# Features dealt to partitions by four, in a kernel of attention with memory beside a SiLU layer

## The chip, the cores and the metric

The kernel runs on one core of a Trainium2 chip. The metric is device time in microseconds (us), from one launch. Five engines have their own instruction queues: TensorE (PE in the profile; its weight loads are PEld), VectorE (DVE), ScalarE (ACT), GpSimd (POOL) and SyncE (SP), which issues most of the DMAs.

## What is computed

The input x has 2048 rows of 512 features in bf16. Each row is normed, and two layers read the normed rows:

```python
xn = _layernorm(x, axis=-1)
return x + _A_ref(xn, A_wq, A_wk, A_wv, A_wo, A_beta) + _B_ref(xn, B_w1, B_w2)

# A: 32 heads of 16, 4 segments of 512 rows; in each segment, with M and z summed over the segments before
q, k, v = xn @ wq, xn @ wk, xn @ wv                 # split in heads and segments
p = softmax(q @ k.T * scale + mask);  a_dot = p @ v
a_mem = (phi(q) @ M) / (phi(q) @ z + 1e-6)          # phi(t) = t + 1 where t > 0, else exp(t)
o = g * a_mem + (1 - g) * a_dot                     # g = sigmoid(beta), one value a head
M += phi(k).T @ v;  z += phi(k).sum(rows)
# A's result is o @ wo;  B's is silu(xn @ w1) @ w2, w1 of 512x1792
```

A sum over the 512 features of xn is the same in whatever order the features are taken, as long as xn and the rows of the weight are in the same order. The change rests on this.

## The kernel before

Rows of x are taken in 16 tiles of 128 rows; four tiles make a segment. All weights stay in SBUF. A product over 512 features takes four steps of 128 features, one feature to a partition, so that both sides are stored as 128 partitions by 4 chunks. `xnT` holds the normed rows turned that way, for all 2048 rows; `wq_sb`, `wk_sb`, `wv_sb` and `w1_sb` hold the weights. Feature f stands at partition f modulo 128 in chunk f div 128. A load of wk (L168 to L174) thus moves, for each partition, four rows of the weight that lie 128 rows apart: runs of 1 KB. wv comes in two loads of two chunks. w1 comes in two halves of its columns (L176 to L180), in runs of 1792 bytes.

The path of a tile into `xnT`:

- sums of the row on VectorE (L286, L289);
- one over the root of the variance: for tiles 0 to 3 on ScalarE and VectorE (L303, L306), one tile at a time; for later tiles four at a time on GpSimd (L297, L300);
- the norm, `ln_norm` (L313 to L318), one VectorE instruction that reads 128x512 bf16 and writes the tile `xn_t`;
- the turn. Tiles 0 to 3 go through TensorE: `turn_mm` (L840 to L845) makes four transposes of 128x128 into PSUM, and `turn_copy` (L847) copies the result to `xnT` on ScalarE or VectorE. Tiles 4 to 15 are turned by a DMA that SP issues, `turn_far` (L856, L857).

After that come the products of q, k, v and h (h is the layer with w1), in `product` (L333 to L343): one instruction over the whole array (L336), or four on 32 columns each (L338). Scores go to PSUM (L724), ScalarE makes their exponentials (L730), GpSimd clears what the mask takes away (L744), and L791 sums v with them. GpSimd also splits k into even and odd heads (L385). VectorE copies the products out of PSUM (L376 for k, L399 for q, L406 for v, L821 and L828 for the weighed sums) and multiplies h by its gate (L497), each of which frees one of the four PSUM banks that these products share.

The order of all this is written out by hand in the string `ORDER` (L16 to L90): words that are run one after the other, so that each engine's queue has its instructions in that order. `Nv6` is the norm of tile 6 on VectorE, `XD6` its turn by DMA, `X0.1` a turn on TensorE, `h0.2.0` a part of a product of h for segment 0, `hv0.0` its gating, `kp0.1` a split of k on GpSimd. The norms stand in this order there:

```text
Nv0 .. Nv1 .. Nv2 .. Nv3 (start)   Nv6 Nv4 XD6 XD4 .. Nv5 XD5 (behind S2, S1)   Nv7 (S3)
Nv8 Nv10 XD8 (S10)   Nv9 Nv11 XD11 (S13)   Nv15 XD15 (S24)   Nv14 (S18)   Nv12 .. Nv13 (S23, S30)
```

At the start SP issues tiles 0 and 2 of x, the two loads of wv, wk, wq, tiles 4 to 7 of x, the two halves of w1, and the rest of x; ScalarE issues tiles 1 and 3, and much later w2 and wo.

Of the kernel before, what the change touches and what calls it, by code (L numbers as in the profile page):

```python
# [93 lines left out]
def kernel(  # L94
# [13 lines left out]
    nc = tc.nc  # L108

    P = 128  # L110
    S = 2048
    D = 512
    DT = D // P
# [5 lines left out]
    TPS = L // P  # L119
# [24 lines left out]
    def xs(t0, t1):  # L144
        if t0 >= NT - TPS:
            return x_end[:, t0 - NT + TPS : t1 - NT + TPS, :]
        return x_lo[:, t0:t1, :] if t1 <= TPS else x_hi[:, t0 - TPS : t1 - TPS, :]

    w1_sb = cpool.tile([P, DT, F], BF16, name="w1_sb")
    w2_sb = cpool.tile([P, FT, D], BF16, name="w2_sb")  # L150
    wk_sb = cpool.tile([P, DT, D], BF16, name="wk_sb")
    wq_sb = cpool.tile([P, DT, D], BF16, name="wq_sb")
    wv_sb = cpool.tile([P, DT, D], BF16, name="wv_sb")
# [3 lines left out]
    def load_x(eng, t0, n):  # L157
        eng.dma_start(
            out=xs(t0, t0 + n),
            in_=x_flat[t0 * P : (t0 + n) * P, :].rearrange("(n p) d -> p n d", p=P),  # L160
        )
# [6 lines left out]
    def load_w(eng, w_sb, W, k0, k1):  # L168
        eng.dma_start(out=w_sb[:, k0:k1, :], in_=W.rearrange("(ko ki) n -> ki ko n", ki=P)[:, k0:k1, :])

    load_w(nc.sync, wv_sb, A_wv, 0, 2)
    load_w(nc.sync, wv_sb, A_wv, 2, 4)
    load_w(nc.sync, wk_sb, A_wk, 0, 4)
    load_w(nc.sync, wq_sb, A_wq, 0, 4)  # L174
    load_x(nc.sync, 4, 4)
    for half in range(2):  # L176
        cols = slice(half * F // 2, (half + 1) * F // 2)
        nc.sync.dma_start(
            out=w1_sb[:, :, cols], in_=B_w1.rearrange("(ko ki) n -> ki ko n", ki=P)[:, :, cols]
        )  # L180
    load_x(nc.sync, 8, 4)
    load_x(nc.sync, 12, 4)
# [1 line left out]
        out=beta_r[:], in_=bass.AP(tensor=A_beta.tensor, offset=A_beta.offset, ap=[[1, H], [0, 4], [1, 1]])  # L184
# [6 lines left out]
    ident = cpool.tile([P, P], BF16, name="ident")  # L191
    make_identity(nc, ident[:])
    Vzs = []
    for i in range(2):
# [6 lines left out]
        out=b16[:], in_=ones8[:], compare_op=ALU.is_ge, fill=0.0,  # L201
# [3 lines left out]
        out=b16[:], in_=b16[:], compare_op=ALU.is_ge, fill=0.0,  # L205
# [73 lines left out]
    mv_all = cpool.tile([P, NT, nc.vector.BN_AGGR_DIM], F32, name="mv_all")  # L279
    rstd_all = cpool.tile([P, NT, 1], F32, name="rstd_all")  # L280
# [30 lines left out]
    xn = {}  # L311

    def ln_norm(t, eng):  # L313
        xn[t] = work.tile([P, D], BF16, name="xn_t", tag="x_res", bufs=4)
        eng.tensor_scalar(
            out=xn[t][:], in0=xs(t, t + 1)[:, 0, :], scalar1=mv_all[:, t, 0:1], scalar2=rstd_all[:, t, 0:1],
            op0=ALU.subtract, op1=ALU.mult,
        )  # L318

    def bank(shape, dtype, name):  # L320
        return pp.tile(shape, dtype, name=name, tag="pb")
# [518 lines left out]
    def turn_mm(t, n):  # L840
        ptr = xn["ptr", t] = bank([P, DT, n, P], BF16, "ptr")
        for i in range(n):
            xn_t = xn.pop(t + i)
            for dt in range(DT):
                nc.tensor.transpose(ptr[:, dt, i, :], xn_t[:, dt * P : (dt + 1) * P], ident[:])  # L845

    def turn_copy(t, n, copy):  # L847
        ptr, parts = xn.pop(("ptr", t)), 2 if t < 2 else 1
# [12 lines left out]
    def keep_busy(n):  # L861
# [23 lines left out]
        "sh": half_store, "xl": load_res, "st": out_store,  # L885
        "xs": ln_stats, "xc": ln_sums, "xd": ln_var, "xg": ln_root, "xq": ln_sqrt, "xi": ln_inv, "tb": first_exp,
        "Nv": lambda t: ln_norm(t, nc.vector), "Na": lambda t: ln_norm(t, nc.gpsimd),
        "X": turn_mm, "XD": turn_far, "Xv": lambda t, n: turn_copy(t, n, vec), "Xa": lambda t, n: turn_copy(t, n, act),
        "odd": make_odd, "bmask": make_bmask, "kind": make_kind, "tanh": make_tanh, "gate": make_gate,
        "zeros": make_zeros, "ones": lambda i: nc.gpsimd.memset(Vzs[i][:, :, :, 1, :], 1.0),  # L890
# [52 lines left out]
```

## Time and profile before

| | |
|---|---|
| median of 3 runs | 220.99 us (220.85 to 221.06) |
| the profiled execution | 220.8 us |
| its span, first to last instruction | 219.1 us |
| TensorE, VectorE, ScalarE, GpSimd busy | 211.6, 181.0, 184.2, 126.8 us |
| TensorE's granted clock | 1.000 of full speed |

A profile is one execution. "Busy" counts the time in which an engine has an instruction running. A group's row names line, engine and operation, then output and inputs by the program's names, shapes and count, and the mean time of one. A row of the timeline starts with the start time and the time taken, both in us from the start of the span; in brackets stands how long the engine was idle before, and what ended that. L with a number is a line of the kernel.

### The profile page before, as it was taken

The numbers are of one execution on the slowest core, as the hardware profiler recorded it, in microseconds if no ns is written. First come the engines' busy times: TensorE is split into PE (matmuls) and PEld (weight loads), VectorE is DVE, ScalarE is ACT, GpSimd is POOL, SyncE is SP. The second block draws the span as 40 slices with busy tenths as digits, with TensorE's granted clock in tenths as the row PEclk, the third lists the DMA queues.
The fourth block names the chain that finished last, engine by engine and source line by source line (L and its number), as shares of the span: only waits on it lengthen the run. The fifth ranks groups of instructions, "written<-read, shape, count | busy, mean of one in ns | idle before, by whom it ended". The sixth has DMA issues, their size and how long they took to land.

```text
span 219.1 us, 9343 instructions
## 1 busy us (share of the span) xinstructions
PE 211.6 (97%) x4019; PEld 116.3 (53%) x4042; DVE 181.0 (83%) x370; ACT 184.2 (84%) x173; POOL 126.8 (58%) x203
## 2 busy tenths in 40 slices
PE   7999999999999999999999999999999999999994
PEld 7666655556544544445544445455454544465663
DVE  7899999999897878757988979777899798669364
ACT  3899989999999999999999999999999988860000
POOL 6039986679687845695845486667768473410000
PEclk9999999999999999999999999999999999999999
DMA  6994549242003035321122142160032221322313
GB/s 197 357 372 128 79 129 344 42 79 46 4 4 75 25 86 71 83 62 29 51 74 61 43 121 28 47 79 7 4 99 75 75 76 45 97 60 76 97 52 97
DMA packets 33273, 19.60 MB, mean 89 GB/s; under 512 B 14672, under 2 KB 33232, under 8 KB 33232
## 3 DMA queue, kind: packets, MB, share of 16 engines
q1 hardware_dynamic: 30608, 16.39, 29.1%
q10 hardware_dynamic: 2624, 2.62, 3.7%
q8 instruction: 31, 0.51, 1.0%
q14 instruction: 10, 0.08, 0.1%
HBM read 9.96 MB, written 2.10 MB: 55 GB/s over the span
## 4 chain that ended last, share of the span: by engine, by line
PE 82%; DVE 9%; POOL 4%; issue 2%; ACT 1%
PE ps L336 20%; PE psO L338 16%; PE ps L338 15%; PE psS L724 9%; PE psO L336 9%; PE psV L791 8%; PE psS L338 4%; DVE stats L286 2%; POOL Pb L744 2%; DVE Vz L406 1%; POOL k L385 1%; DVE hT L497 1%; DVE pk L433 1%; POOL lows L744 1%; PE ptr L845 1%
## 5 line engine op out<-in xcount | busy, mean ns | idle before, releaser
L730 ACT ACTIVATE Pb<-psS 128x2048 bf16<-128x2048 f32 x72 | 135.2, 1877 | 6.3 <-PE psS L724 4.1
L744 POOL TENSOR_SCALAR_AFFINE_SELECT Pb<-Pb 128x512 bf16<-128x512 bf16 (+2 forms) x88 | 61.6, 710 | 19.2 <-ACT Pb L730 16.5
L497 DVE SCALAR_TENSOR_TENSOR hT<-th,ps 128x512 bf16<-128x512 bf16 x56 | 38.0, 681 | 10.6 <-ACT th L492 10.2
L744 POOL TENSOR_SCALAR_AFFINE_SELECT lows<-Pb 64x512 bf16<-64x512 bf16 (+1 forms) x40 | 23.2, 581 | 37.5 <-ACT Pb L730 31.1
L338 PE MATMUL psO<-w_sb,hT 128*32 128x512 bf16 (+2 forms) x708 | 43.3, 321 | 0.0
L336 PE MATMUL ps<-xnT,w_sb 128*128 128x512 bf16 (+1 forms) x165 | 34.2, 329 | 0.4 <-DVE Vz L406 0.2
L492 ACT ACTIVATE th<-ps 128x512 bf16<-128x512 f32 x56 | 33.2, 594 | 1.7 <-PE ps L338 1.6
L338 PEld LDWEIGHTS <-hT 128*32 128x32 bf16 x876 | 21.6, 97 | 14.0 <-issue 2.6
L338 PE MATMUL ps<-xnT,w_sb 128*32 128x512 bf16 (+1 forms) x448 | 26.4, 348 | 0.0
L724 PE MATMUL psS<-qT,k 32*128 32x64 bf16 (+3 forms) x512 | 23.0, 233 | 0.5 <-ACT Pb L730 0.3
L336 PEld LDWEIGHTS <-w_sb 128*128 128x128 bf16 x168 | 15.8, 98 | 11.4 <-issue 1.0
L791 PE MATMUL psV<-Pb,Vz 128*32 128x448 bf16 (+7 forms) x512 | 21.6, 286 | 0.2 <-POOL Pb L744 0.2
L724 PEld LDWEIGHTS <-k 32*128 32x128 bf16 x512 | 9.4, 92 | 22.8 <-issue 22.2
L336 PE MATMUL psO<-w_sb,hT 128*128 128x512 bf16 (+2 forms) x82 | 20.9, 326 | 0.6 <-issue 0.5
L791 PEld LDWEIGHTS <-Vz 128*32 128x32 bf16 x768 | 16.2, 97 | 9.2 <-issue 0.8
L621 DVE SCALAR_TENSOR_TENSOR o_out<-psO,x_res 128x512 bf16<-128x512 f32 x14 | 9.6, 689 | 6.6 <-PE psO L338 4.9
L338 PEld LDWEIGHTS <-w_sb 128*32 128x32 bf16 x448 | 11.2, 96 | 7.3 <-issue 1.6
L724 PE MATMUL psS<-qT,kT 16*128 16x448 bf16 (+3 forms) x256 | 14.7, 269 | 0.0
L821 DVE CAST oraw<-psV 128x512 bf16<-128x512 f32 x15 | 10.2, 682 | 3.1 <-PE psV L791 3.0
L406 DVE CAST Vz<-ps 128x512 bf16<-128x512 f32 x15 | 10.2, 682 | 2.8 <-PE ps L338 1.6
L336 PEld LDWEIGHTS <-hT 128*128 128x128 bf16 x89 | 7.8, 98 | 8.7 <-issue 2.2
L336 PE MATMUL ps<-xnT,wq_sb 128*128 128x256 bf16 (+1 forms) x59 | 12.1, 322 | 0.2 <-issue 0.2
(113 smaller groups left out, 333.5 us busy)
## 6 DMA issues: line engine op xcount, KB each, us to landing
spr<-rz SPq DMA_DIRECT2D x56, 64.0 KB
x_res<-in_A_x_dram SPq DMA_DIRECT2D x16, 128.0 KB
out_dram<-o_out SPq DMA_DIRECT2D x15, 128.0 KB
w_sb<-in_B_w_dram SPq DMA_DIRECT2D x2, 896.0 KB
w_sb<-in_B_w_dram ACTq DMA_DIRECT2D x1, 1792.0 KB
x_hi<-in_A_x_dram SPq DMA_DIRECT2D x2, 512.0 KB
wv_sb<-in_A_wv_dram SPq DMA_DIRECT2D x2, 256.0 KB
wk_sb<-in_A_wk_dram SPq DMA_DIRECT2D x1, 512.0 KB
```

Of the source, the lines that this page charges most:

```text
L286: nc.vector.bn_stats(out=stats[t][:], in_=xs(t, t + 1)[:, 0, :])
L336: return [nc.tensor.matmul(out, lhsT=lhsT, rhs=rhs, start=start, stop=stop, skip_group_check=True)]
L338: nc.tensor.matmul(out[c : c + 32], lhsT=lhsT[:, c : c + 32], rhs=rhs, start=start, stop=stop, tile_position=(0, c), skip_group_check=True,)
L406: copy(out=Vzs[s % 2][:, j, :, 0:3:2, :], in_=sts[s].pop(("v", j))[:, :].rearrange("p (h r d) -> p h r d", r=2, d=DH),)
L492: nc.scalar.activation(out=th[:], in_=sts[s]["h", ft][:, :], func=AF.Tanh, scale=0.5)
L497: nc.vector.scalar_tensor_tensor(out=st["hT"][:, ft, :], in0=st.pop(("th", ft))[:], scalar=1.0, in1=st.pop(("h", ft))[:, :], op0=ALU.add, ...
L621: out = nc.vector.scalar_tensor_tensor(out=o_out[:], in0=st.pop(("psO", j)), scalar=0.5, in1=st["x", j][:], op0=ALU.mult, op1=ALU.add)
L724: nc.tensor.matmul(psS[:, g, c : c + q2 - q1], lhsT=keys[rows], rhs=st["qT"][rows, dt, q1:q2], start=True, stop=True, tile_position=(32 * ...
L730: exp = nc.scalar.activation(out=blocks(Pb, b).rearrange("p y g c -> p g y c"), in_=psS[:, :, :].rearrange("p g (y c) -> p g y c", c=BLOCK ...
L744: over[id(Pb)].append(nc.gpsimd.affine_select(out=out, in_=in_, compare_op=ALU.is_ge, fill=0.0, base=base, pattern=[[0, out.shape[1]], [1, ...
L791: nc.tensor.matmul(psV[32 * g : 32 * g + 32, q0 : q0 + nq].rearrange("p (y c) -> p y c", y=weights.shape[2]), lhsT=Vzs[s % 2][:, kt, 4 * d ...
L821: copy(out=oraw[:], in_=sts[s].pop(("psV", 0))[:, :])
```

## The change

The features are dealt out by four: feature f stands at partition f div 4, in chunk f modulo 4. Partition p then holds rows 4p to 4p + 3 of a weight, which lie side by side in memory. wk and wq so come in runs of 4 KB, and each load of wv, of two chunks, in runs of 2 KB. w1 is dealt in the same way, but comes in halves of its columns, so its runs stay at 1792 bytes. w2 and wo, which are not multiplied with xn, keep the old function.

`xnT` has to follow. For tiles 0 to 3 the norm stays, and each transpose on TensorE reads every fourth column of the normed tile in place of 128 neighbours. For tiles 4 to 15 the turn by DMA stays, and the norm on VectorE deals the features: it reads its row of x with a step of four elements and writes the 512 results side by side, in the new order.

```diff
+    def load_wx(eng, w_sb, W, k0, k1):
+        eng.dma_start(out=w_sb[:, k0:k1, :], in_=W.rearrange("(ki ko) n -> ki ko n", ki=P)[:, k0:k1, :])
+
-    load_w(nc.sync, wv_sb, A_wv, 0, 2)
-    load_w(nc.sync, wv_sb, A_wv, 2, 4)
-    load_w(nc.sync, wk_sb, A_wk, 0, 4)
-    load_w(nc.sync, wq_sb, A_wq, 0, 4)
+    load_wx(nc.sync, wv_sb, A_wv, 0, 2)
+    load_wx(nc.sync, wv_sb, A_wv, 2, 4)
+    load_wx(nc.sync, wk_sb, A_wk, 0, 4)
+    load_wx(nc.sync, wq_sb, A_wq, 0, 4)
...
-            out=w1_sb[:, :, cols], in_=B_w1.rearrange("(ko ki) n -> ki ko n", ki=P)[:, :, cols]
+            out=w1_sb[:, :, cols], in_=B_w1.rearrange("(ki ko) n -> ki ko n", ki=P)[:, :, cols]
...
     def ln_norm(t, eng):
         xn[t] = work.tile([P, D], BF16, name="xn_t", tag="x_res", bufs=4)
+        to, frm = xn[t][:, :], xs(t, t + 1)[:, 0, :]
+        if t >= TPS:
+            to, frm = to.rearrange("p (k c) -> p k c", k=DT), frm.rearrange("p (c k) -> p k c", k=DT)
         eng.tensor_scalar(
-            out=xn[t][:], in0=xs(t, t + 1)[:, 0, :], scalar1=mv_all[:, t, 0:1], scalar2=rstd_all[:, t, 0:1],
+            out=to, in0=frm, scalar1=mv_all[:, t, 0:1], scalar2=rstd_all[:, t, 0:1],
             op0=ALU.subtract, op1=ALU.mult,
         )
...
-                nc.tensor.transpose(ptr[:, dt, i, :], xn_t[:, dt * P : (dt + 1) * P], ident[:])
+                nc.tensor.transpose(ptr[:, dt, i, :], xn_t[:, dt:D:DT], ident[:])
```

## The prediction

> **What bounds the kernel now.** I read the page first, then busy time by stretch, then who waited for whom in the start, then single instructions round each norm.
>
> ```profile
> span 219.1 us, 9343 instructions
> PE 211.6 (97%) x4019; PEld 116.3 (53%) x4042; DVE 181.0 (83%) x370; ACT 184.2 (84%) x173; POOL 126.8 (58%) x203
> ```
>
> TensorE is busy for 211.6 of 219.1 us, so 7.5 us is all that waiting costs today. The change adds and removes no product. It can only move the time by making TensorE wait longer or less. The profiled execution took 220.8 us (the span and 1.7 us around it); the median of the runs shown is 220.99, which is 0.19 more.
>
> The busy time by stretch (stretch, length, then busy us of PE, PEld, DVE, ACT, POOL, then clock, DMA share, GB/s) shows what is tight where:
>
> ```profile
> 5.00:9.00 4.00, 3.46 (x35) 2.00 (x34) 3.72 (x15) 2.89 (x9) 0.00 (x0) 1.00 1.02 338
> 10.00:14.00 4.00, 3.84 (x41) 3.12 (x39) 3.22 (x8) 3.71 (x6) 0.77 (x1) 1.00 1.07 382
> 21.00:27.00 6.00, 5.74 (x108) 3.86 (x109) 5.43 (x11) 5.95 (x7) 5.60 (x9) 1.00 0.62 90
> 27.00:38.00 11.00, 10.72 (x204) 5.79 (x204) 10.82 (x22) 10.02 (x11) 8.20 (x13) 1.00 0.74 224
> 46.00:52.00 6.00, 5.97 (x185) 3.46 (x182) 5.59 (x12) 5.95 (x6) 5.76 (x9) 1.00 0.41 70
> ```
>
> In 27 to 38 VectorE has 0.18 us of air in 11, TensorE 0.28. In 46 to 52 TensorE has 0.03 us in 6. The DMA engines are full in the first 14 us. Whether somebody waits for them is told by the waits of TensorE and its weight loads between 5 and 16 us:
>
> ```profile
> PE ptr L845 <- DVE xn_t L315: 0.3, 1, 0.3
> PE psS L724 <- ACT qT L399: 0.2, 1, 0.2
> ```
>
> ```profile
> PEld L845 <- DVE xn_t L315: 1.0, 3, 0.5
> PEld L336 <- ACT xnT L851: 0.8, 2, 0.5
> ```
>
> Every named wait is for a norm (L315) or for a copy out of PSUM (L851, L399). None is for a DMA.
>
> **The loads: 0.** wv, wk and wq are first read here (start, busy time, engine, line):
>
> ```profile
> 6.46 0.11 PEld L336 LDWEIGHTS <-xnT 128*128 128x128 bf16 x2 [0.30 <-ACT xnT L851]
> 8.37 0.37 PEld L336 LDWEIGHTS <-wk_sb 128*128 128x128 bf16 x4
> 10.11 0.86 PEld L336 LDWEIGHTS <-wq_sb 128*128 128x128 bf16 x8
> ```
>
> The product with wv starts when ScalarE's copy ends; those with wk and wq carry no idle time at all. So a load that lands earlier has nobody to release. Nor is it clear that it lands much earlier: 338 GB/s moved in 5 to 9 us, where rows of 1 KB come in, and 382 in 10 to 14, where the 1792-byte runs of w1 take over. The three weights are 1.57 MB: 4.65 us at the one rate, 4.12 at the other, so at most 0.53 us for the last. The bounds are 0 and a gain of 0.53; I take 0, since no row shows a wait that this would shorten. x_hi, w1 and the later rows of x keep their run lengths and come as many as before; SP issues the same DMAs in the same order, so no queue is passed. If the runs are cut into 1 KB pieces all the same, this term stays 0.
>
> **The transposes of the first four tiles: 0.** Sixteen weight loads now read every fourth element.
>
> ```profile
> L845 PEld LDWEIGHTS <-xn_t x16: 95/98/99, 5.6 to 9.0; 128*128 128x128 bf16 x16
> 5.60 0.23 PEld L845 LDWEIGHTS <-xn_t 128*128 128x128 bf16 x4 [0.49 <-DVE xn_t L315]
> ```
>
> Four of them take 0.23 us, one following the other after 0.04. Nothing in this trace loads with a step. Between no change and a load that no longer overlaps the next one (4 x 0.098 = 0.39, so 0.16 more for a tile, 0.64 for four) I take 0, by the row itself. The cover is thin, as TensorE waits for the norm before its tiles and the copies wait for TensorE; the upper end stays in the range.
>
> **The norms of tiles 4 to 15: +0.5.** Tiles 0 to 3 keep their norm as it is. The other twelve read with a step of four. What they take now (ns, min/median/max), and three rows that bear on the rate:
>
> ```profile
> L315 DVE TENSOR_SCALAR xn_t<-x_hi,mv_all,rstd_all x8: 396/406/787, 18.3 to 44.6; 128x512 bf16<-128x512 bf16 x8
> L315 DVE TENSOR_SCALAR xn_t<-x_lo,mv_all,rstd_all x4: 413/414/414, 5.1 to 8.4; 128x512 bf16<-128x512 bf16 x4
> L315 DVE TENSOR_SCALAR xn_t<-x_end,mv_all,rstd_all x4: 632/714/773, 64.1 to 89.5; 128x512 bf16<-128x512 bf16 x4
> ```
>
> ```profile
> L392 DVE TENSOR_SCALAR k<-kT,pm_odd 128x512 bf16<-128x512 bf16 x1 | 0.4, 353 | 0.6 <-ACT kT L376 0.6
> L527 DVE TENSOR_SCALAR zsum<-ps,evec 128x256 f32<-128x256 f32 x1 | 0.5, 484 | 0.0
> L566 DVE TENSOR_SCALAR rz<-ri,gate 32x256 bf16<-32x256 f32 x1 | 0.4, 352 | 0.0
> ```
>
> All three are the same operation with one scalar column. 256 fp32 elements out of PSUM take 484 ns, 256 fp32 elements out of SBUF 352, and 512 bf16 elements out of SBUF 353. So SBUF gains 0.13 us on 256 elements, and packed bf16 passes twice as many in the same time. I read this as one, two and four elements a cycle, with 0.13 us for 128 cycles. Bf16 with gaps between its elements can't be packed, as fp32 can't. Its nearest row is L566: two a cycle, 0.414 + 0.13 = 0.54 us. The ends: 0.41 if nothing is lost, 0.414 + 3 x 0.13 = 0.81 at one a cycle. I take 0.54, so 12 x 0.13 = 1.6 us more of VectorE. What of it reaches TensorE goes by place.
>
> Place A, tiles 6, 4, 5, then 7:
>
> ```profile
> 18.34 1.59 DVE L315 TENSOR_SCALAR xn_t<-x_hi,mv_all,rstd_all 128x512 bf16<-128x512 bf16 x3
> 18.49 0.81 POOL L385 TENSOR_SCALAR k<-kT,pm_odd 128x512 bf16<-128x512 bf16 x1
> 20.44 0.40 DVE L315 TENSOR_SCALAR xn_t<-x_hi,mv_all,rstd_all 128x512 bf16<-128x512 bf16 x1
> 20.91 0.60 PE L336 MATMUL ps<-xnT,w_sb 128*128 128x256 bf16 x4
> 21.11 1.35 DVE L399 CAST qT<-ps 128x512 bf16<-128x512 f32 x2 [0.27 <-PE ps L336]
> 25.49 0.61 PE L338 MATMUL ps<-wv_sb,xnT 128*32 128x512 bf16 x8
> 26.73 0.29 PE L791 MATMUL psV<-Pb,Vz 128*32 128x256 bf16 x4 [0.20 <-POOL Pb L744]
> 27.07 0.69 DVE L821 CAST oraw<-psV 128x512 bf16<-128x512 f32 x1 [0.47 <-PE psV L791]
> ```
>
> ```profile
> L385 POOL TENSOR_SCALAR k<-kT,pm_odd x15: 688/693/1017, 18.5 to 163.0; 128x512 bf16<-128x512 bf16 x15
> ```
>
> Behind the first three norms stands the gating product of h that frees a PSUM bank, done by 20.44; the next product of h starts at 20.91. That is 0.47 us of cover for 3 x 0.13 = 0.39. With the fourth norm VectorE is 0.52 late, of which its idle 0.27 at 21.11 takes half and the 0.47 at 27.07 the rest. The first transpose of these tiles is issued 0.13 later; the product that first reads its tile runs at 25.49, more than 5 us after, and is covered. What isn't covered is GpSimd. Its split of k at 18.49 took 0.81 us beside the norms, while the median of such splits is 0.69; and one of the norms took 0.787, so the two hold each other up. GpSimd is busy for 5.60 of the 6 us from 21 to 27, and at 26.73 TensorE waits for it. One or two norms longer by 0.13 ahead of GpSimd's two splits give 0.13 to 0.26; I take **0.2**.
>
> Place B, tiles 8 and 10, then 9, then 11:
>
> ```profile
> 41.52 0.73 DVE L315 TENSOR_SCALAR xn_t<-x_hi,mv_all,rstd_all 128x512 bf16<-128x512 bf16 x2
> 43.07 0.69 DVE L497 SCALAR_TENSOR_TENSOR hT<-th,ps 128x512 bf16<-128x512 bf16 x1 [0.22 <-ACT th L492]
> 43.67 0.45 DVE L315 TENSOR_SCALAR xn_t<-x_hi,mv_all,rstd_all 128x512 bf16<-128x512 bf16 x1
> 44.64 0.40 DVE L315 TENSOR_SCALAR xn_t<-x_hi,mv_all,rstd_all 128x512 bf16<-128x512 bf16 x1
> 51.83 0.23 DVE L464 COPY M<-psM 128x64 f32<-128x64 f32 x1 [0.37 <-PE ps L338]
> ```
>
> The first pair costs 0.26 and meets 0.22 of idle time; the next two add 0.26. VectorE is then 0.3 us late until its next idle time at 51.83, through the copies of q and k that free the banks, in a stretch where TensorE has 0.03 us of air. I take all of it, **0.3**; the ends are 0 (the banks come free early enough) and 0.5.
>
> Place C, tiles 12 to 15:
>
> ```profile
> 66.31 0.69 DVE L399 CAST qT<-ps 128x512 bf16<-128x512 f32 x1 [0.22 <-PE ps L336]
> 68.70 0.69 DVE L376 CAST kT<-ps 128x512 bf16<-128x512 f32 x1 [0.27 <-PE ps L336]
> 79.06 0.69 DVE L497 SCALAR_TENSOR_TENSOR hT<-th,ps 128x512 bf16<-128x512 bf16 x1 [0.33 <-ACT th L492]
> 91.01 0.69 DVE L497 SCALAR_TENSOR_TENSOR hT<-th,ps 128x512 bf16<-128x512 bf16 x1 [0.81 <-ACT th L492]
> ```
>
> Two norms run at 64 and 65 us, one at 76, one at 89. Each is followed by idle time of at least its 0.13. I take 0, at most 0.1.
>
> The sum is 0 + 0 + 0.2 + 0.3 + 0 = 0.5 us: 221.3 against the profiled 220.8, and 221.5 as a median of runs.
>
> [...]
>
> **The rivals.**
>
> *Faster, 220.5.* The place is the start, the mechanism the landing of wv, wk and wq. A wait is put down to the event that came last; if a weight in truth lands a moment behind the copy that is named, 4 KB runs move it forward. The price: TensorE idles 0.54 us in 5 to 9, and 0.53 is what the faster rate could bring, so -0.5, with the norms hidden. It decides from the point where wk lands after 8.37 or wq after 10.11. For it: DMA share of 1.02. Against it: no wait is put down to a DMA, and both weight loads start without idle time.
>
> *The strided read is slower still, 222.1.* The norm stands between 0.54 and 0.81; in the middle, 0.68, each costs 0.27. A: three make 0.81 against 0.47 of cover, 0.34 late, and some 0.1 for the fourth. B: four make 1.08, less 0.22, of which some 0.6 reaches TensorE before the idle 0.37. C: 0.1. Together 1.1. [...] For it: the step leaves one used element in 8 bytes. At one element a cycle (0.40 each) the same working gives 0.9 + 1.0 + 0.3 = 2.2, 223.2.
>
> *No difference, 221.0.* TensorE's banks and queue ahead take up VectorE's 0.3 in B, and GpSimd is not held longer in A. For it: VectorE is busy for only 83% of the span. Against it: 0.03 us of air.
>
> **How the numbers follow.** The bound is 0.2%, 0.44 us, which is about what a measurement of this kernel can tell from no change: 220.55 to 221.43. Forecast 45%, its own range 221.1 to 222.0; 31 of these lie above the bound and 14 within it. Faster rival 18%, slower read 12%, one a cycle 10%, no difference 15%. Faster: 0.18. Same: 0.14 + 0.15 = 0.29. Slower: 0.31 + 0.22 = 0.53. The range 220.5 to 222.6 holds all but the fastest part of the first rival and the case of one a cycle; the 0.64 for the transposes, on top of the forecast, lies in it.
>
> **What would show it.** The norms of tiles 4 to 15 at about 0.54 us where GpSimd is quiet, those of tiles 0 to 3 at 0.41; weight loads at L845 still near 98 ns; the first products with wv, wk and wq at the same instants; TensorE's idle time up by 0.2 by 27 us and by 0.3 more by 52. The prediction is wrong if the first products with wk or wq start earlier without an earlier copy ahead of them, if the norms take 0.7 or more, or if TensorE's idle time up to 52 us is what it was.

## The result, and the profile after

The changed kernel takes 222.97 us as a median of four runs (222.86 to 223.29), the kernel before 221.03 beside it. The ratio is 1.0091, with a 95% interval of 1.0073 to 1.0108: 1.94 us slower. The profiled execution after took 223.29 us, 2.49 more than that of before; it is the longest of the four, and 0.46 us of what follows is a later start, of which more below.

From the page after, the span, the busy times and the DMA packets; below them the packets of before:

```profile
span 221.6 us, 9343 instructions
PE 212.1 (96%) x4019; PEld 116.4 (53%) x4042; DVE 184.1 (83%) x370; ACT 184.2 (83%) x173; POOL 128.0 (58%) x203
DMA packets 32249, 19.60 MB, mean 88 GB/s; under 512 B 14672, under 2 KB 31696, under 8 KB 32208
```

```profile
DMA packets 33273, 19.60 MB, mean 89 GB/s; under 512 B 14672, under 2 KB 33232, under 8 KB 33232
```

The loads do what they say: 1536 packets of 1 KB have become 256 of 2 KB and 256 of 4 KB, 1024 fewer in all. TensorE does the same work: its busy time is 0.5 us longer (212.1 us against 211.6), its idle time 2.0 (9.5 against 7.5). VectorE is busy for 3.1 us more, where the prediction had 1.6.

Every VectorE instruction stands in the same place of its queue in both kernels, so the start times can be set side by side. Timeline rows after, and those of before that were not shown yet:

```profile
10.88 0.58 ACT L383 CAST kT<-ps 128x512 bf16<-128x512 f32 x1 [0.54 <-PE ps L343]
18.79 2.00 DVE L322 TENSOR_SCALAR xn_t<-x_hi,mv_all,rstd_all 128x512 bf16<-128x512 bf16 x3
28.09 0.69 DVE L828 CAST oraw<-psV 128x512 bf16<-128x512 f32 x1
42.01 0.69 DVE L383 CAST kT<-ps 128x512 bf16<-128x512 f32 x1
54.24 0.23 DVE L471 COPY M<-psM 128x64 f32<-128x64 f32 x1 [0.23 <-PE psM L459]
81.56 0.69 DVE L504 SCALAR_TENSOR_TENSOR hT<-th,ps 128x512 bf16<-128x512 bf16 x1 [0.19 <-ACT th L499]
218.08 0.97 DVE L675 SCALAR_TENSOR_TENSOR o_half<-psS,x_res 128x256 bf16<-128x256 f32 x2 [0.18 <-PE psS L345]
```

```profile
10.42 0.59 ACT L376 CAST kT<-ps 128x512 bf16<-128x512 f32 x1 [0.26 <-PE ps L336]
40.91 0.69 DVE L376 CAST kT<-ps 128x512 bf16<-128x512 f32 x1
215.59 0.97 DVE L668 SCALAR_TENSOR_TENSOR o_half<-psS,x_res 128x256 bf16<-128x256 f32 x2 [0.18 <-PE psS L338]
```

The lag of the changed kernel at these rows is 0.46, 0.45, 1.02, 1.10, 2.41, 2.50 and 2.49 us. It grows in three steps: 0.46 in the start, 0.6 across the norms of tiles 4 to 7, 1.3 across those of tiles 8 to 11. Behind 54 us, with four norms still to come, it hardly moves.

TensorE's own waits between 14 and 55 us name two instructions of VectorE that were not there before, hT and qT (us in total, times, longest):

```profile
PE ps L343 <- DVE hT L504: 1.3, 1, 1.3
PE psS L731 <- ACT Pb L737: 0.6, 2, 0.3
PE ps L343 <- DVE qT L406: 0.5, 1, 0.5
```

In the same stretch before:

```profile
PE psS L724 <- ACT Pb L730: 0.3, 1, 0.3
PE psV L791 <- POOL Pb L744: 0.2, 1, 0.2
PE ps L336 <- DVE Vz L406: 0.2, 1, 0.2
```

The first of the two places, tiles 4 to 7, in the timeline after:

```profile
18.79 2.00 DVE L322 TENSOR_SCALAR xn_t<-x_hi,mv_all,rstd_all 128x512 bf16<-128x512 bf16 x3
18.95 0.94 POOL L392 TENSOR_SCALAR k<-kT,pm_odd 128x512 bf16<-128x512 bf16 x1
21.30 1.44 DVE L322 TENSOR_SCALAR xn_t<-x_hi,mv_all,rstd_all 128x512 bf16<-128x512 bf16 x1
21.37 1.09 POOL L751 TENSOR_SCALAR_AFFINE_SELECT Pb<-Pb 128x1024 bf16<-128x1024 bf16 x1
22.66 1.27 DVE L406 CAST qT<-ps 128x512 bf16<-128x512 f32 x2
23.39 0.81 PE L343 MATMUL ps<-wv_sb,xnT 128*128 128x512 bf16 x2 [0.48 <-DVE qT L406]
```

The norm of tile 7 takes 1.44 us. It starts 0.07 us ahead of a selection of GpSimd (the instruction that clears what the mask takes away) and ends 0.28 us behind it. In the kernel before it took 0.40 at 20.44, and the same selection came 0.14 us later, at 20.58:

```profile
20.58 1.21 POOL L744 TENSOR_SCALAR_AFFINE_SELECT Pb<-Pb 128x1024 bf16<-128x1024 bf16 x1
44.93 0.96 POOL L744 TENSOR_SCALAR_AFFINE_SELECT lows<-Pb 64x512 bf16<-64x512 bf16 x1 [0.96 <-ACT Pb L730]
44.96 0.43 DVE L835 COPY_PREDICATED oraw<-omask,odd 128x256 int32<-128x256 int32 x1
```

There it was GpSimd that gave way: its selections took 1.21 and 0.96 us in place of the usual 1.09 and 0.66. The second place after, tiles 8 to 11:

```profile
44.77 0.80 DVE L322 TENSOR_SCALAR xn_t<-x_hi,mv_all,rstd_all 128x512 bf16<-128x512 bf16 x1
46.02 0.66 POOL L751 TENSOR_SCALAR_AFFINE_SELECT lows<-Pb 64x512 bf16<-64x512 bf16 x1 [0.73 <-ACT Pb L737]
46.09 0.87 DVE L322 TENSOR_SCALAR xn_t<-x_hi,mv_all,rstd_all 128x512 bf16<-128x512 bf16 x1
46.75 1.16 POOL L751 TENSOR_SCALAR_AFFINE_SELECT Pb<-Pb 128x1024 bf16<-128x1024 bf16 x1
46.88 1.32 DVE L842 COPY_PREDICATED oraw<-omask,odd 128x256 int32<-128x256 int32 x1
48.10 0.67 DVE L504 SCALAR_TENSOR_TENSOR hT<-th,ps 128x512 bf16<-128x512 bf16 x1
48.83 1.02 PE L343 MATMUL ps<-xnT,wk_sb 128*128 128x512 bf16 x4 [1.29 <-DVE hT L504]
```

Two norms are held up, at 44.77 and 46.09: 0.80 and 0.87 us, where 0.54 is the time of an undisturbed one. What is held up most is not a norm. It is the merge of odd heads behind them, which copies the sums of the odd heads to their place and which the change doesn't touch: 0.43 us before, 1.32 now. Behind it in VectorE's queue waits the gating of h, and TensorE waits 1.29 us for that.

Last, the instructions that the change altered (ns, min/median/max):

```profile
L322 DVE TENSOR_SCALAR xn_t<-x_hi,mv_all,rstd_all x8: 536/747/1436, 18.8 to 46.1; 128x512 bf16<-128x512 bf16 x8
L322 DVE TENSOR_SCALAR xn_t<-x_lo,mv_all,rstd_all x4: 412/413/414, 5.3 to 8.6; 128x512 bf16<-128x512 bf16 x4
L322 DVE TENSOR_SCALAR xn_t<-x_end,mv_all,rstd_all x4: 762/848/908, 66.6 to 92.0; 128x512 bf16<-128x512 bf16 x4
L852 PEld LDWEIGHTS <-xn_t x16: 111/113/131, 5.8 to 9.5; 128*128 128x128 bf16 x16
```

A stepped norm that nobody disturbs takes 0.536 us. The median of the first eight is 0.747, because five of them run beside GpSimd and take 0.69 us or more.

### The profile page after: what moved, and what is told of

It reads as the page before. It is cut to its first block, busy times and chain, and to the rows that moved or that the text cites. A ratio compares the mean times of both kernels' runs of the same rounds, so it can differ in the third digit from the quotient of the medians.

```text
span 221.6 us, 9343 instructions
## 1 busy us (share of the span) xinstructions
PE 212.1 (96%) x4019; PEld 116.4 (53%) x4042; DVE 184.1 (83%) x370; ACT 184.2 (83%) x173; POOL 128.0 (58%) x203
## 4 chain that ended last, share of the span: by engine, by line
PE 82%; DVE 9%; DMA 5%; issue 2%; ACT 1%
PE ps L343 19%; PE psO L345 16%; PE ps L345 15%; PE psS L731 10%; PE psO L343 9%; PE psV L798 8%; DMA x_hi<-in_A_x_dram 4%; PE psS L345 4%; DVE xn_t L322 3%; DMA x_lo<-in_A_x_dram 1%; DVE stats L290 1%; DVE qT L406 1%; ACT Pb L737 1%; DVE hT L504 1%; DVE Vz L413 1%
## 5 line engine op out<-in xcount | busy, mean ns | idle before, releaser
L392 POOL TENSOR_SCALAR k<-kT,pm_odd 128x512 bf16<-128x512 bf16 x15 | 11.3, 756 | 2.5 <-DVE kT L383 1.6
L343 PE MATMUL ps<-wv_sb,xnT 128*128 128x512 bf16 x41 | 11.5, 380 | 1.0 <-DVE qT L406 0.5
```

The lines of the kernel that those rows point to most:

```text
L343: return [nc.tensor.matmul(out, lhsT=lhsT, rhs=rhs, start=start, stop=stop, skip_group_check=True)]
L392: nc.gpsimd.tensor_scalar(out=to, in0=frm, scalar1=keep[:, 0:1], scalar2=1.0, op0=ALU.mult, op1=ALU.mult)
```

## The experiments

Two theories at first. **P**: the longer norms bring VectorE and GpSimd together at two places, where one waits for a whole instruction of the other. **L**: the loads cost what is lost, since the lag begins in the start. A third, **the rate alone**: twelve norms 0.13 us longer, each passed on in part.

### The three parts alone

Loads only (the changed kernel with the norms and transposes of before), transposes only, norms only (each is the kernel before with that one part of the change), and loads with transposes. In these the features of xn and the rows of the weights no longer match, for some tiles or for all, so only the time counts.

```diff
 # loads only
-        if t >= TPS:
+        if False:
...
-                nc.tensor.transpose(ptr[:, dt, i, :], xn_t[:, dt:D:DT], ident[:])
+                nc.tensor.transpose(ptr[:, dt, i, :], xn_t[:, dt * P : (dt + 1) * P], ident[:])
```

> Only the weights are dealt by four; norms and transposes stay as before, so the rows of a weight meet other features than in the reference. Theory P (the time is lost where VectorE and GpSimd hold each other up behind the longer norms): no wait of that kind can arise, so 0 to +0.5 us against before, all of it in the first 12 us. Theory L (the loads cost what is lost, since wk and wq end later than with 1 KB runs): +0.4 to +1 us, with TensorE waiting for wk at its first product. The rival of the prediction (longer runs land earlier and release TensorE): -0.2 to -0.5 us.

> Only the four transposes of each of the tiles 0 to 3 read every fourth column; weights stay as before, so the first segment's features are not paired as in the reference. In the changed kernel a weight load of these took 113 ns in place of 98. Theory P and theory L: 0 to +0.1 us, as 15 ns times 16 is 0.24 us and most of it lies beside waits for the norm. A theory that the transposes cost the start: +0.3 us or more.

> Only the norms of tiles 4 to 15 read with a step; weights stay as before, so segments 2 to 4 do not pair features as in the reference. Theory P: +1.3 to +2.2 us, most of the 1.94, in two steps behind the norms of tiles 4 to 7 and 8 to 11, with single VectorE instructions of over 1 us there. Theory L: +0.5 us or less. A theory of the rate alone (12 times 0.13 us, each passed on in part): +0.3 to +0.8 us, and no instruction over 1 us.

> The change without the step in the norms; tiles 4 to 15 are then not paired as in the reference. Theory P: 0 to +0.5 us against before. Theory L: +0.8 us or more.

| kernel | median, us | ratio to before | 95% interval |
|---|---|---|---|
| loads only | 221.16 | 0.9997 | 0.9989 to 1.0006 |
| transposes only | 221.08 | 1.0000 | 0.9989 to 1.0010 |
| norms only | 223.01 | 1.0088 | 1.0075 to 1.0101 |
| loads and transposes | 221.05 | 0.9999 | 0.9989 to 1.0009 |

The norms are the whole of it. Theory L falls: packets of 2 and 4 KB change nothing that a run shows, in either direction, and so the faster rival of the prediction falls too. The lag of 0.46 in the start is the spread of single executions. The copy of v ahead of the first of these norms starts at 17.74 us before and at 18.19 after; with the new loads it starts at 17.77 in the kernel with both moves below, with the old ones at 18.46 in that with three pauses, ahead of the first pause. In the profile after, TensorE's weight loads wait once for wk, 0.3 us. They do not in the profiles of loads only and of loads with transposes, which have the same loads, so the wait comes with single executions and not with the length of the runs.

### By place

```diff
 # against norms only
-        if t >= TPS:
+        if TPS <= t < 2 * TPS:        # the other kernel: 2 * TPS <= t < 3 * TPS
```

> The kernel before, with the step in the norms of tiles 4 to 7 only (their segment is then not paired as in the reference). Theory P, by the lag of the changed kernel behind the one before at this place (0.46 us ahead of it, 1.10 behind it): +0.6 us, with the norm of tile 7 at over 1 us beside a selection of GpSimd. Theory of the rate alone (4 of 12 norms): a third of the whole, +0.65, but no instruction over 1 us and no single wait of TensorE over 0.3.

> The same with the step in the norms of tiles 8 to 11 only. Theory P, by the lag at this place (1.10 ahead of it, 2.48 behind it): +1.3 us, with the merge of the odd heads behind the norm of tile 11 held up to over 1 us; less, if the lag from tiles 4 to 7 is needed to bring the two together. Theory of the rate alone: +0.65 us.

Tiles 4 to 7 alone: 221.74 us, ratio 1.0022 (1.0008 to 1.0037), beside 221.10 for before. Tiles 8 to 11 alone: 222.55, ratio 1.0063 (1.0044 to 1.0081). The two differences of medians, 0.64 and 1.45 us (by the ratios 0.5 and 1.4), make 2.09; all twelve made 1.94 and 1.95. So nothing that the runs show is left for tiles 12 to 15, and each place costs its own share without the other. A theory of the rate alone had 0.65 for either: 1.45 speaks against it, 0.64 by itself does not. The long instructions, which it did not have, are there in each, first the timeline of tiles 4 to 7 alone, then that of tiles 8 to 11 alone:

```profile
21.25 1.44 DVE L318 TENSOR_SCALAR xn_t<-x_hi,mv_all,rstd_all 128x512 bf16<-128x512 bf16 x1
```

```profile
46.20 1.32 DVE L838 COPY_PREDICATED oraw<-omask,odd 128x256 int32<-128x256 int32 x1
```

### Moving what is held up

The changed kernel with a word of `ORDER` moved, so that the instruction that is held up has nobody behind it whom TensorE waits for.

```diff
 # norm of tile 7
-S3 ... q0.2.3 Nv7 qv0.2 ha0.1 ...      S4 qv0.3 hv0.1 XD7 ...
+S3 ... q0.2.3 qv0.2 ha0.1 ...          S4 qv0.3 hv0.1 Nv7 XD7 ...
 # merge of odd heads
-... h0.9.1 Om1 h0.9.2 h0.9.3 h0.10.0 ha0.9 hv0.9 kv1.2 kp1.2
+... h0.9.1 h0.9.2 h0.9.3 h0.10.0 ha0.9 hv0.9 kv1.2 Om1 kp1.2
```

> The changed kernel with one word of the order moved: the norm of tile 7 goes behind the copies of q and the gating of h that stood behind it, so that these do not wait when GpSimd holds it up. The same instructions at the same rate. Theory P: 0.4 to 0.7 us less than the changed kernel, 222.3 to 222.6. Theory of the rate alone: as the changed kernel, 222.8 to 223.1, since VectorE has the same work.

> The changed kernel with the merge of odd heads (the instruction that took 1.32 us in place of 0.43) moved behind the gating of h and the copy of k that stood behind it. Theory P: 0.9 to 1.4 us less than the changed kernel, 221.6 to 222.1. Theory of the rate alone: as the changed kernel, 222.8 to 223.1.

> The changed kernel with both moves (norm of tile 7, merge of odd heads). Theory P: the two savings add up, 0.3 + 1.0 below the changed kernel, 221.5 to 221.8, so 0.5 to 0.8 above before; what is left is the first three norms, which hold up GpSimd's splits, and 0.13 us a norm. Theory of the rate alone was not borne out by the single moves; by it nothing would change.

> The kernel before with the same two moves: what the moves do by themselves. Theory P: -0.2 to +0.2 us, since there neither instruction is held up for long. If the moves were a gain of their own: -0.3 us or more, and the savings in the changed kernel would not be put down to the meeting with GpSimd.

| kernel | median, us | ratio to before | 95% interval |
|---|---|---|---|
| changed, norm of tile 7 moved | 222.65 | 1.0075 | 1.0057 to 1.0094 |
| changed, merge moved | 221.99 | 1.0034 | 1.0024 to 1.0044 |
| changed, both moved | 221.63 | 1.0021 | 1.0006 to 1.0035 |
| before, both moved | 221.36 | 1.0002 | 0.9986 to 1.0017 |

The same instructions at the same rate, and 1.4 of the 1.94 us are gone (0.51 are left); in the kernel before the moves gain nothing. The merge is the larger part, as expected. With it alone moved, its own row in the timeline is back to 0.44 us:

```profile
46.31 1.16 POOL L751 TENSOR_SCALAR_AFFINE_SELECT Pb<-Pb 128x1024 bf16<-128x1024 bf16 x1
47.64 0.44 DVE L842 COPY_PREDICATED oraw<-omask,odd 128x256 int32<-128x256 int32 x1
```

The norm of tile 7 gave back less than the 0.4 to 0.7 us expected: 0.32 by the medians, and 0.36 where the merge is moved too. Each time the intervals of the two kernels compared overlap, so its size is not sure. With it out of the way TensorE waits for GpSimd once between 14 and 56 us, 0.2 us, as in the kernel before (at 26.73). GpSimd is late at the first place: its two splits beside the first three norms took 0.94 and 0.63 us, against 0.81 and 0.50 before. The timeline of GpSimd with both moved:

```profile
18.53 0.94 POOL L392 TENSOR_SCALAR k<-kT,pm_odd 128x512 bf16<-128x512 bf16 x1
19.45 0.63 POOL L392 TENSOR_SCALAR k<-kT,pm_even 128x256 bf16<-128x256 bf16 x1
```

### Late, or longer

Is it enough that VectorE comes later, or does it take the longer norm? The kernel before, with norms as short as they were, and small instructions of 0.112 us behind each of the twelve.

```diff
             op0=ALU.subtract, op1=ALU.mult,
         )
+        if t >= TPS:
+            for _ in range(2):        # 1, 2 or 3
+                eng.memset(ident[:], 0.0)
```

> The kernel before, its norms without the step, but each of the twelve is followed by a small instruction that takes VectorE 0.1 to 0.14 us (it clears the identity, which nobody reads any more). If the loss is a matter of when VectorE's instructions meet GpSimd's, whatever made them late: +1.0 to +2.2 us, with the same two instructions held up. If it takes the longer hold of the stepped norm itself: 0 to +0.6 us.

> As the kernel with a pause, but two small instructions behind each norm, since one of them only moved the next instruction by 0.03 to 0.07 us. Wanted are some 0.1 to 0.2 us of delay a norm, as much as the step costs. If being late is enough: +1.0 to +2.2 us, the norm of tile 7 or the merge of odd heads held up to over 1 us. [...]

> The same with three, so that the delay of the step lies between the two or below. If being late is enough: +1.0 to +2.5 us. If it takes the longer norm itself: up to +0.8 us, growing with the delay and without an instruction of over 1 us at the two places.

One pause: 221.35 us, ratio 1.0009 (0.9993 to 1.0024). Two: 222.70, ratio 1.0062 (1.0043 to 1.0081). Three: 224.08, ratio 1.0117 (1.0092 to 1.0141). One pause came out as expected if it takes the longer norm. But it moved the next instruction by only 0.03 to 0.07 us, half of what the step adds or less; two moved it by 0.26, twice the step. Between the two lies the edge, and the timeline shows it. With one pause, VectorE then GpSimd:

```profile
20.72 0.40 DVE L315 TENSOR_SCALAR xn_t<-x_hi,mv_all,rstd_all 128x512 bf16<-128x512 bf16 x1
45.32 0.83 DVE L837 COPY_PREDICATED oraw<-omask,odd 128x256 int32<-128x256 int32 x1
```

```profile
20.83 1.23 POOL L746 TENSOR_SCALAR_AFFINE_SELECT Pb<-Pb 128x1024 bf16<-128x1024 bf16 x1
45.21 0.65 POOL L746 TENSOR_SCALAR_AFFINE_SELECT lows<-Pb 64x512 bf16<-64x512 bf16 x1 [0.96 <-ACT Pb L732]
```

With two:

```profile
20.93 1.12 DVE L315 TENSOR_SCALAR xn_t<-x_hi,mv_all,rstd_all 128x512 bf16<-128x512 bf16 x1
46.41 1.12 DVE L838 COPY_PREDICATED oraw<-omask,odd 128x256 int32<-128x256 int32 x1
```

```profile
20.81 1.09 POOL L747 TENSOR_SCALAR_AFFINE_SELECT Pb<-Pb 128x1024 bf16<-128x1024 bf16 x1
46.14 1.09 POOL L747 TENSOR_SCALAR_AFFINE_SELECT Pb<-Pb 128x1024 bf16<-128x1024 bf16 x1
```

With one pause the norm of tile 7 starts 0.11 us ahead of the selection and takes its 0.40, and GpSimd pays 0.14. With two it starts 0.12 us behind it and takes 1.12. The merge slides from the short selection, which costs it 0.4, onto the long one, which costs it 0.7. With three, the 2.55 us lie just above the upper end of what was expected, and at the second place another instruction loses. The norm of tile 11 waits, and the merge behind it is short:

```profile
47.13 1.10 DVE L315 TENSOR_SCALAR xn_t<-x_hi,mv_all,rstd_all 128x512 bf16<-128x512 bf16 x1
48.62 0.45 DVE L838 COPY_PREDICATED oraw<-omask,odd 128x256 int32<-128x256 int32 x1
```

So being late is enough: a plain norm that comes too late loses as the stepped one does (1.12 us with two pauses, 1.44 with the step). No run makes a plain norm late by just the 0.13 us of the step. That the longer norm, besides, holds GpSimd up is seen in the splits above; how much of the 0.5 us left with both moves is due to that was not told apart.

### The same idea on the kernel before

One sum of the feature map takes 1.03 us at 28.9 us, beside a split of k, where its median is 0.69. It was moved behind two instructions that free banks for TensorE.

```diff
-... vv1.2 fv0.3 O0 Ov0    S11 lw0 hv0.2 xs11 ...
+... vv1.2 O0 Ov0          S11 lw0 hv0.2 fv0.3 xs11 ...
```

> The kernel before with one sum of the feature map (1.03 us at 28.9 us beside a split of k, where its median is 0.69) moved behind two instructions that free banks for TensorE. Theory P, applied to the kernel before: -0.1 to -0.4 us. If the stretch is bound otherwise: 0.

221.47 us, ratio 1.0014 (0.9999 to 1.0029): no gain, where 0.1 to 0.4 was expected. TensorE's waits between 14 and 55 us are the three of before, 0.3, 0.2 and 0.2. In these runs moving a long instruction from beside GpSimd gained only where the profile showed TensorE waiting behind it (0.5 and 1.3 us in the profile after), and the profile of before shows no such wait here. No kernel of the study beats the one before.

## Why the prediction was wrong, point by point

**The loads at 0: right.** The run with the loads alone gives 0.9997, and in its profile no weight load waits for wk. From 5 to 9 us the DMAs moved 371 GB/s in the profile after and 338 before, as that rival had it, and it made no difference. Busy time by stretch after, where the last number was 338 before:

```profile
5.00:9.00 4.00, 3.21 (x30) 1.79 (x29) 3.71 (x15) 2.72 (x10) 0.00 (x0) 1.00 0.99 371
```

**The transposes at 0: right.** Their weight loads take 113 ns in place of 98, 16 x 15 ns = 0.24 us in all; alone they give 1.0000.

**The stepped norm at 0.54 us: right.** It takes 0.536 and 0.541 where GpSimd is quiet (tiles 8 and 10), against 0.412 to 0.414 for the plain norms of tiles 0 to 3, so the 0.13 us taken from the row of fp32 held. No norm of before reads with a step of four. That the step costs bf16 its faster rate was the author's estimate, and the runs show it as this difference of 0.12 us. The rates in elements a cycle are a reading of three rows; the profiles give lengths alone. The slower read falls, though its 222.1 lies nearer to the result.

**Place C at 0: right**, as the lag does not grow behind 54 us.

**Places A and B: wrong in size, by the same failed step.** In A the prediction let the fourth norm's lateness vanish in VectorE's idle 0.27 and 0.47 us, and charged GpSimd with 0.2. In B it took VectorE to be "0.3 us late until its next idle time" and passed on all of that. Both sums add lengths: an instruction of 0.13 us more makes what follows 0.13 later, at most. The trace of before had shown that norms and GpSimd's instructions hold each other up, and the prediction said so, but it charged only a longer norm's 0.13 to GpSimd. It never asked what happens when the other engine becomes the one that waits. Measured, A costs 0.64 and B 1.45 us, against 0.2 and 0.3. In B the merge comes to stand behind a selection of 1.16 us, and moving it gave back some 1.0. In A the lead that the norm of tile 7 had on a selection of 1.09 us shrank from 0.14 to 0.07, and the norm took 1.44 us and ended 0.28 behind it. Moving it gave back some 0.3. The rest in A stands beside GpSimd's lateness, which the prediction had seen, but whose share no run measured by itself. The price was in the trace of before: 1.09 us for a selection, and 0.787 for a norm that had met a split of 0.81. With both moves 0.5 us are left, which is the prediction's sum; that it is made up of the same parts is not shown.

By what means the two engines hold each other up, no profile says; the rows show lengths and times. The merge went from 0.43 to 1.32 us beside a selection of 1.16. The order of the starts alone doesn't settle who waits, as the norm that began 0.07 us ahead of the selection still ended 0.28 behind it.

## What to carry to other kernels

Where a timeline shows two engines holding each other up, as VectorE and GpSimd here, a small change of length can have a price that jumps: look for how far the earlier of the two starts ahead of the other, and charge most of the other's length if the change eats into that lead. Here a stepped norm took 0.9 us more beside a selection of 1.09. The lead was 0.14 us; 0.11 was still enough, 0.07 was not. Then look at who stands behind the loser in its queue; moving the loser behind those whom the bound engine waits for cost nothing here and gave back 1.4 of 1.94 us. And longer runs in the loads were worth nothing here, where no wait of the profile before named a load, although the DMA engines had a busy share of 1.02 from 5 to 9 us and 1.07 from 10 to 14.

## What the runs showed of the hardware

A weight load of 128x128 bf16 that reads every fourth element took 113 ns in the median of sixteen (111 to 131 in the profile after), one that reads neighbours 98 (95 to 99 before). A small instruction of 0.112 us on VectorE moved the next one by 0.03 to 0.07 us when it stood alone, and a second one behind it by some 0.2 more, so the length of such a row is not what it cost the queue here.
